# A run of small TensorE products and of other engines' operations behind the last store of an mLSTM and MLP kernel

## The chip, the cores and the metric

The kernel runs on one core of one Trainium2 chip. The metric is the device time of one execution in microseconds, the median of the runs. In the tables and rows PE is TensorE, PEld its weight loads, DVE VectorE, ACT ScalarE, POOL GpSimd and SP the engine that issues the DMAs.

## The reference

Two stages follow each other. The first is a gated recurrence per batch (4), head (8) and step (768), head size 40, here cut to its loop:

```python
for t in range(S):
    m_new = np.maximum(f_gate[:, :, t] + m, i_gate[:, :, t])
    f_stab = np.exp(f_gate[:, :, t] + m - m_new)
    i_stab = np.exp(i_gate[:, :, t] - m_new)
    C = f_stab * C + i_stab * np.einsum('bhd,bhe->bhde', vt, kt)
    n = f_stab * n + i_stab * kt
    y[:, :, t] = sigmoid(o_gate) * (C @ qt) / np.maximum(np.abs(n . qt), 1.0)
```

Its output, laid out as 3072 tokens of 320 values, goes through an MLP: `h = x @ w_in` (320 to 2048), `g = h * clip(h + 3, 0, 6) / 6`, and `g @ w_out` (2048 to 320), which is the result.

## The kernel before

The recurrence is computed in chunks of 128 steps, and three chunks of one batch make a unit of 384 tokens; there are eight units. For a unit, two tasks of four heads each compute scores (`s`), decays (`gw`), the products with the values (`o`) and the running state (`C`). Small fp32 products stand there at the start of the program: `s` in line 659 (40 rows of the array in use, 128 columns of weights, 128 streamed), `o` in lines 701 and 708 (42 columns streamed) and the state's `c` in line 581 (40 columns of weights, 42 streamed). Later tasks use bf16 pieces instead (lines 662, 703 to 711). Products of zeros (`pw`, line 359) fill PE's gaps until the first unit is done.

A unit then goes through the MLP. `mm1` (line 877) makes the 16 blocks of the hidden layer, each from eight fp32r products of 384 streamed columns, into two PSUM buffers `mm0` and `mm1`. ACT and DVE make `g`, then its high and low parts `gh` and `gl` in fp32r. `mm2` (lines 920 to 922) adds the products of 320 columns into `acc0` to `acc2`. `evac` copies each `acc` to one of three SBUF buffers `ob0` to `ob2`, on ACT, DVE and ACT in turn (lines 940 and 937), and SP stores it (line 943).

The order of each engine's instructions is set ahead by a planner (`Plan`), which gives every step costs and due times and emits the steps in the order that it simulates. `plan.run()` emits all of them; each engine then executes its list in that order, and semaphores make it wait for what it needs from another. At the program's end all engines meet in closing steps.

The last steps of the program are the last `mm2` of unit 7 on PE, the three copies of `acc`, and the three stores. The change calls a function behind `plan.run()`. It uses buffers that the kernel has: `g0` and `gl0` for its operands, `mm0`, `mm1` and the `acc` buffers for its results in PSUM, and `ob0` in SBUF.

Of the kernel before, what the change touches and what calls it, by code (L numbers as in the profile page):

```python
# [7 lines left out]
F32 = mybir.dt.float32  # L8
F32R = mybir.dt.float32r
BF16 = mybir.dt.bfloat16  # L10
U32 = mybir.dt.uint32
AF = mybir.ActivationFunctionType
ALU = mybir.AluOpType
# [3 lines left out]
DM, FF = 320, 2048  # L17
# [11 lines left out]
NEG = -1.0e30  # L29
# [59 lines left out]
class Mat(float):  # L89


    w = 0.0
# [18 lines left out]
class Plan:  # L111
# [21 lines left out]
    def put(self, tag, slot):  # L133
        self.slots[tag].append((self.now["t"], slot))
# [152 lines left out]
def mlstm_moe_kernel(ctx: ExitStack, tc: tile.TileContext, ig, fg, qkd, natd, ond, w_in, w_out, ident_d, out):  # L287
    nc = tc.nc
# [10 lines left out]
    whi = wts.tile([128, 2, FF], F32R, name="whi")  # L299
# [4 lines left out]
    ident = cst.tile([128, 128], F32, name="ident")  # L304
    ones = cst.tile([128, max(WN, 128)], BF16, name="ones")
    half = cst.tile([128, 1], F32, name="half")
# [23 lines left out]
    def pick(i, due=0.0, **costs):  # L330
        opts = {e: costs[e] for e in {"x": "dg", "y": "da", "z": "dga", "p": "g"}.get(ENGINES[i], ENGINES[i]) if e in costs}
        return ("*", opts, due) if len(opts) > 1 else (*list(opts.items())[0], due)
# [10 lines left out]
    def psub(i, n, g=None, due=0.0):  # L343
        return pick(i, due, d=ld(n), g=g or cg(n))

    def pcast(i, n, due=0.0):
        return pick(i, due, a=ca(n), d=lf(n))
# [503 lines left out]
    P = {}  # L851
# [77 lines left out]
    def evac(u, t):  # L929
# [13 lines left out]
        nc.sync.dma_start(out[t0 + t * L : t0 + (t + 1) * L, :], ob)  # L943
        put(*got)

    def due(u, k):
        if u == 1:
            return T0 + SPAN * (k + 1) / 7 - AH1
        return T0 + SPAN * (u - 1) + SPAN * (k + 1) / 7 - AH
# [8 lines left out]
    for task in range(2 * NU):  # L958
# [3 lines left out]
        k = quad * U  # L962
# [44 lines left out]
            plan.add(T0 + SPAN * u + SPAN - MV, evac(u, t), [f"acc{u}_{t}"])  # L1007
    with tc.manual_schedule(engines={ET.PE, ET.Activation, ET.DVE, ET.Pool, ET.SP}):
        plan.run()


_INS = ["ig", "fg", "qk", "nat", "on", "w_in", "w_out", "ident"]
# [49 lines left out]
```

## Time and profile before

| what | value |
|---|---|
| median of the timed runs | 576.79 us (576.59 to 576.99) |
| the profiled execution, first to last instruction (span) | 591.0 us |
| PE busy | 540.3 us, 91% of the span |
| PEld busy | 493.6 us |
| DVE busy | 404.1 us |
| ACT busy | 337.8 us |
| POOL busy | 141.0 us |
| mean granted TensorE clock | 0.913 of full speed |

The profiled execution has no other time than its span, and it is 14.2 us longer than the median of the timed runs. Matmuls are pipelined: a row's duration reaches from a product's start until its results are written, and the next one starts before that, so PE's rate is read from the distance between starts. An fp32 product (plain fp32) stands in the trace as two MATMULs, one in fp32r as one, and a weight load stands beside each as PEld. A row of the timeline merges neighbours of the same line (x8). The granted clock is the share of TensorE's clock pulses that were let through.

### The profile page before, as it was taken

What the parts mean: (1) busy time and instruction counts of PE and PEld (TensorE: products, weight loads), DVE (VectorE), ACT (ScalarE), POOL (GpSimd) and SP (SyncE); (2) the same over time, 40 slices, a digit from 0 to 9 for tenths busy, and PEclk for the clock granted to TensorE, in tenths of its full rate; (3) what the DMA queues carried; (4) which work ended last, traced back from release to release, by engine and by line L of the source; (5) the groups of instructions that cost most, each with busy time, mean ns of one, the idle gap of its engine ahead of it and who ended that gap; (6) DMA issues with size and microseconds to landing.
All of it is one profiled execution on the core that took longest, in us unless ns stands there. A gap on an engine that the chain in (4) does not pass through costs nothing.

```text
span 591.0 us, 11413 instructions
## 1 busy us (share of the span) xinstructions
PE 540.3 (91%) x4207; PEld 493.6 (84%) x4207; DVE 404.1 (68%) x849; ACT 337.8 (57%) x738; POOL 141.0 (24%) x191
## 2 busy tenths in 40 slices
PE   8999999687799897999789997999978998999997
PEld 7988899476679797889678896999868997999997
DVE  6443476997588767779767775796957677685433
ACT  4521164474746756667666666676756567544433
POOL 3242111543530312221211322132212203110000
PEclk9555588788999999999889998999989999999999
DMA  8524137549316226253454135344534244300000
GB/s 280 145 74 154 41 109 192 159 149 259 123 48 180 96 77 180 83 145 97 140 178 143 37 112 158 105 136 139 155 112 144 67 123 140 123 15 34 1 1 34
DMA packets 34548, 69.26 MB, mean 117 GB/s; under 512 B 4301, under 2 KB 14725, under 8 KB 34493
## 3 DMA queue, kind: packets, MB, share of 16 engines
q1 hardware_dynamic: 34493, 68.54, 38.0%
q8 instruction: 33, 0.54, 0.4%
q14 instruction: 22, 0.18, 0.1%
HBM read 42.66 MB, written 4.03 MB: 79 GB/s over the span
## 4 chain that ended last, share of the span: by engine, by line
PE 57%; DMA 16%; DVE 12%; ACT 7%; SPq 3%; issue 2%; POOL 1%; DVEq 0%; POOLq 0%; ACTq 0%
PE h L877 20%; DMA gw<-gsc 6%; PE acc L920 5%; PE acc L922 5%; PE acc L921 5%; PE pw L359 3%; DMA nat<-in_nat_dram 3%; PE o L701 3%; PE s L659 2%; DMA qk<-in_qk_dram 2%; PE c L581 2%; PE o L708 2%; PE s L662 2%; DMA rawi<-in_w_in_dram 2%; PE acc L918 2%
## 5 line engine op out<-in xcount | busy, mean ns | idle before, releaser
L877 PE MATMUL h<-xh,whi 128*128 128x384 f32 x256 | 95.4, 373 | 17.9 <-DVE g L893 17.8
L893 DVE SCALAR_TENSOR_TENSOR g<-g,h 128x384 f32<-128x384 f32 x128 | 70.1, 551 | 60.3 <-ACT g L891 59.7
L920 PE MATMUL acc<-vh,gh 128*128 128x320 f32 x336 | 108.6, 323 | 1.4 <-ACT gh L339 1.4
L891 ACT ACTIVATE g<-h,half 128x384 f32<-128x384 f32 x128 | 73.6, 576 | 57.4 <-PE h L877 49.7
L922 PE MATMUL acc<-vh,gl 128*128 128x320 f32 x336 | 104.1, 310 | 0.1
L921 PE MATMUL acc<-vl,gh 128*128 128x320 f32 x336 | 104.1, 310 | 0.0
L877 PE MATMUL h<-xl,whi 128*128 128x384 f32 x256 | 88.7, 347 | 0.0
L877 PE MATMUL h<-xh,wlo 128*128 128x384 f32 x256 | 88.7, 346 | 0.0
L642 ACT ACTIVATE gw<-gw,cT 128x128 f32<-128x128 f32 x192 | 65.4, 393 | 32.9 <-POOL gw L637 32.8
L637 POOL TENSOR_SCALAR_AFFINE_SELECT gw<-gw 128x512 f32<-128x512 f32 x46 | 33.2, 722 | 187.8 <-DMA gw<-gsc 144.1
L901 DVE TENSOR_TENSOR gl<-g,gh 128x384 fp32r<-128x384 f32 x112 | 63.8, 573 | 19.0 <-ACT gh L339 18.3
L339 ACT CAST gh<-g 128x384 fp32r<-128x384 f32 x112 | 57.1, 511 | 30.3 <-DVE g L893 29.5
L877 PEld LDWEIGHTS h<-xh,whi 128*128 128x128 f32 x256 | 50.2, 196 | 24.0 <-DVE g L893 23.1
L920 PEld LDWEIGHTS acc<-vh,gh 128*128 128x128 f32 x336 | 63.6, 189 | 2.2 <-ACT gh L339 1.9
L922 PEld LDWEIGHTS acc<-vh,gl 128*128 128x128 f32 x336 | 63.4, 189 | 0.6 <-DVE gl L901 0.6
L921 PEld LDWEIGHTS acc<-vl,gh 128*128 128x128 f32 x336 | 63.7, 190 | 0.0
L339 ACT CAST p<-gw 128x512 bf16<-128x512 f32 x72 | 44.2, 614 | 19.7 <-DVE gw L666 13.8
L877 PEld LDWEIGHTS h<-xl,whi 128*128 128x128 f32 x256 | 50.3, 196 | 0.2
L877 PEld LDWEIGHTS h<-xh,wlo 128*128 128x128 f32 x256 | 50.2, 196 | 0.0
L877 PE MATMUL h<-xl,wtl 128*128 128x384 f32 x128 | 45.0, 352 | 0.4 <-DVE xl L784 0.3
L877 PE MATMUL h<-xh,wtl 128*128 128x384 f32 x128 | 44.5, 348 | 0.0
L666 DVE TENSOR_TENSOR gw<-s,gw 128x512 f32<-128x512 f32 x48 | 33.0, 687 | 16.7 <-PE s L662 9.5
(118 smaller groups left out, 1096.8 us busy)
## 6 DMA issues: line engine op xcount, KB each, us to landing
st<-spl SPq DMA_DIRECT2D x117, 160.0 KB
gw<-gsc SPq DMA_DIRECT2D x46, 256.0 KB
nat<-in_nat_dram SPq DMA_DIRECT2D x16, 492.0 KB
qk<-in_qk_dram SPq DMA_DIRECT2D x13, 480.0 KB
rawi<-in_w_in_dram SPq DMA_DIRECT2D x8, 640.0 KB
rawo<-in_w_out_dram SPq DMA_DIRECT2D x8, 640.0 KB
on<-in_on_dram SPq DMA_DIRECT2D x8, 480.0 KB
out_dram<-ob SPq DMA_DIRECT2D x24, 160.0 KB
```

The lines of the kernel that those rows point to most:

```text
L339: nc.scalar.copy(dst, src)
L359: nc.tensor.matmul(pw[:, :WN], ones[:, :128], ones[:, :WN], start=True, stop=True)
L637: nc.gpsimd.affine_select(gw, gw, pattern=[[0, 4], [1, L]], compare_op=ALU.is_ge, fill=NEG, base=0, channel_multiplier=-1)
L642: nc.scalar.activation(gw[:, h, :], gw[:, h, :], AF.Exp, bias=cT[:, c, r0 + h : r0 + h + 1], scale=1.0)
L666: nc.vector.tensor_tensor(gw, sp, gw, ALU.mult)
L877: nc.tensor.matmul(hp, w, x, start=n == 0, stop=n == len(seq) - 1)
L891: nc.scalar.activation(g, hp, AF.Relu, bias=half, scale=1.0 / 6.0)
L893: nc.vector.scalar_tensor_tensor(g, g, 1.0, hp, ALU.min, ALU.mult)
L901: E(e).tensor_sub(gl, g, gh.bitcast(F32))
L920: nc.tensor.matmul(acc, gh[:, ts_], VH[f // 4][:, f % 4, :], start=f == 0, stop=False)
L921: nc.tensor.matmul(acc, gh[:, ts_], VL[p][:, f % 2, :], start=False, stop=False)
L922: nc.tensor.matmul(acc, gl[:, ts_], VH[f // 4][:, f % 4, :], start=False, stop=f == NF - 1)
```

## The change

A function `shapes` is added and called once, behind all steps of the plan. It first copies two pieces of the weights `whi` into SBUF (`sh_src` in fp32, `sh_srr` in fp32r, both on DVE). Then it issues 206 products on PE, in groups that differ in the rows, the weight columns and the streamed columns. Where an operand starts at row 64, or the result at partition 64, the product lies in another part of the array; operands of up to 64 rows or results of up to 64 partitions take a sub-array tile of 64 rows or columns. Behind them six exponentials on ACT, eight operations on POOL and six on DVE write the scratch tile `sh_sc` in `ob0`. Nothing that it writes is stored.

On PE the new rows stand right behind what was the last product, where only the program's closing branch stood. `acc` is the accumulator of the last unit, `shm` are the new results in `mm0` and `mm1`.

```order
 L921 MATMUL acc_2_7030<-vl_2147,gh_15_7312 128x320
 L922 MATMUL acc_2_7030<-vh_2027,gl_15_7313 128x320
-L1057 UNCONDITIONAL_BRANCH
+L956 MATMUL shm_7370<-whi 128x512
+L956 MATMUL shm_7371<-whi 128x512
```

Nothing of before moved; eight more products like the last two follow, then the others. Further down the same list, still on PE, stand the products in column tiles, the transposes, and the first round of those that mix one product of full width with four in 64x64 tiles (`sha` are the new results in the `acc` buffers).

```order
+L956 MATMUL shm_7370<-sh_src 64x128 x8
+L956 MATMUL shm_7370<-sh_src 40x42 x10
+L993 MATMUL shm_7370<-ident,sh_src 128x128 x4
+L956 MATMUL shm_7371<-whi 128x384
+L956 MATMUL sha_7372<-sh_src 64x64 x2
+L956 MATMUL sha_7373<-sh_src 64x64 x2
```

All of these are new rows, and none of them stands ahead of a product of the kernel. On DVE the program ended with the copy of the second accumulator; now the two copies of weights and six operations stand behind it. The last four read PSUM tiles that PE writes (`sha`, `shm`).

```order
 L937 COPY ob_1_7352<-acc_1_7020 128x320
-L1057 UNCONDITIONAL_BRANCH
+L950 COPY sh_src<-whi 128x384
+L951 CAST sh_srr<-whi 128x384
+L1023 TENSOR_TENSOR sh_sc<-sh_src 128x256 x2
+L1025 SCALAR_TENSOR_TENSOR sh_sc<-sh_src,half,sha_7372 128x42 x2
+L1027 TENSOR_TENSOR sh_sc<-sh_src,shm_7370 128x256 x2
+L1141 UNCONDITIONAL_BRANCH
```

The list of DVE ahead of these rows is the one of before. ACT and POOL get their rows at the end of their lists in the same way; SP's list is the same.

```diff
--- before.py
+++ after.py
@@ -943,6 +943,89 @@
         nc.sync.dma_start(out[t0 + t * L : t0 + (t + 1) * L, :], ob)
         put(*got)
 
+    def shapes():
+        mo = P["mo"]
+        src = mo.tile([128, 384], F32, tag="g0", name="sh_src")
+        srr = mo.tile([128, 384], F32R, tag="gl0", name="sh_srr")
+        nc.vector.tensor_copy(src, whi[:, 0, 0:384].bitcast(F32))
+        nc.vector.tensor_copy(srr, whi[:, 0, 512:896].bitcast(F32))
+        bank = [P["mm"].tile([128, 512], F32, tag=f"mm{i}", name=f"shm{i}") for i in range(2)]
+        bank += [P["ac"].tile([128, 512], F32, tag=f"ac{i}", name=f"sha{i}") if False else P["ac"].tile([128, DM], F32, tag=f"acc{i}", name=f"sha{i}") for i in range(3)]
+
+        def mm(out, w, x):
+            nc.tensor.matmul(out, w, x, start=True, stop=True)
+
+        for i in range(10):
+            mm(bank[i % 2], whi[:, 0, i * 128 : i * 128 + 128], whi[:, 1, 0:512])
+        for i in range(8):
+            mm(bank[i % 2][:, :384], whi[:, 0, 0:128], whi[:, 1, 0:384])
+        for i in range(8):
+            mm(bank[2 + i % 2][:, :320], whi[:, 0, 0:128], whi[:, 1, 0:320])
+        for n in (64, 42):
+            for k in range(6):
+                for r in range(2):
+                    for c in range(2):
+                        rows = slice(r * 64, r * 64 + (40 if n == 64 else 64))
+                        mm(bank[r][c * 64 : c * 64 + 64, k * n : k * n + n], src[rows, k % 5 * 64 : k % 5 * 64 + 64], src[rows, 64 : 64 + n])
+        for k in range(8):
+            for r in range(2):
+                mm(bank[r][r * 64 : r * 64 + 64, k * 42 : k * 42 + 42], src[r * 64 : r * 64 + 64, k * 40 : k * 40 + 64], src[r * 64 : r * 64 + 64, 64:106])
+        for k in range(6):
+            for r in range(2):
+                for c in range(2):
+                    mm(bank[r][c * 64 : c * 64 + 40, k * 42 : k * 42 + 42], src[r * 64 : r * 64 + 64, k * 40 : k * 40 + 40], src[r * 64 : r * 64 + 64, 64:106])
+        for k in range(4):
+            for r in range(2):
+                mm(bank[r][:, k * 128 : k * 128 + 128], src[r * 64 : r * 64 + 40, k * 80 : k * 80 + 128], src[r * 64 : r * 64 + 40, 128:256])
+        for k in range(4):
+            for r in range(2):
+                mm(bank[r][:, k * 42 : k * 42 + 42], src[r * 64 : r * 64 + 40, k * 80 : k * 80 + 128], src[r * 64 : r * 64 + 40, 128:170])
+        for k in range(5):
+            for r in range(2):
+                mm(bank[r][:, 0:384], srr[r * 64 : r * 64 + 64, k * 64 : k * 64 + 128], srr[r * 64 : r * 64 + 64, 0:384])
+        for k in range(4):
+            for c in range(2):
+                mm(bank[0][c * 64 : c * 64 + 64, k * 128 : k * 128 + 128], src[:, k * 60 + c * 50 : k * 60 + c * 50 + 64], src[:, 0:128])
+        for k in range(5):
+            for c in range(2):
+                mm(bank[0][c * 64 : c * 64 + 40, k * 42 : k * 42 + 42], src[:, k * 60 + c * 40 : k * 60 + c * 40 + 40], src[:, 0:42])
+        for k in range(4):
+            nc.tensor.transpose(bank[0][:, k * 128 : k * 128 + 128], src[:, k * 80 : k * 80 + 128], ident)
+        for k in range(4):
+            mm(bank[1][:, 0:384], whi[:, 0, k * 128 : k * 128 + 128], whi[:, 1, 0:384])
+            for r in range(2):
+                for c in range(2):
+                    rows = slice(r * 64, r * 64 + 40)
+                    mm(bank[2 + r][c * 64 : c * 64 + 64, k * 64 : k * 64 + 64], src[rows, k * 64 : k * 64 + 64], src[rows, 64:128])
+        for k in range(4):
+            mm(bank[1][:, 0:384], whi[:, 0, k * 128 : k * 128 + 128], whi[:, 1, 0:384])
+            mm(bank[0][:, 0:42], src[:, 0:128], src[:, 0:42])
+            mm(bank[0][:, 42:84], src[:, 0:128], src[:, 0:42])
+        for k in range(4):
+            mm(bank[1][:, 0:384], whi[:, 0, k * 128 : k * 128 + 128], whi[:, 1, 0:384])
+            for r in range(2):
+                mm(bank[2 + r][:, 0:320], srr[r * 64 : r * 64 + 64, 0:128], srr[r * 64 : r * 64 + 64, 0:320])
+        sc = mo.tile([128, DM], F32, tag="ob0", name="sh_sc")[:, :256].rearrange("p (h t) -> p h t", h=4)
+        s4 = src[:, 0:256].rearrange("p (h t) -> p h t", h=4)
+        for h in range(4):
+            nc.scalar.activation(sc[:, h, :], s4[:, h, :], AF.Exp, bias=half, scale=1.0)
+        nc.scalar.activation(sc, s4, AF.Exp)
+        nc.scalar.activation(sc, s4, AF.Exp)
+        for k in range(2):
+            nc.gpsimd.tensor_tensor(sc, s4, src[:, 256:320][:, None, :].broadcast_to([128, 4, 64]), ALU.add)
+        for k in range(2):
+            nc.gpsimd.tensor_tensor(sc, s4, src[:, 256:260][:, :, None].broadcast_to([128, 4, 64]), ALU.add)
+        for k in range(2):
+            nc.gpsimd.affine_select(sc, s4, pattern=[[0, 4], [1, 64]], compare_op=ALU.is_ge, fill=NEG, base=0, channel_multiplier=-1)
+        for k in range(2):
+            nc.gpsimd.tensor_scalar(sc, s4, half, None, ALU.add)
+        for k in range(2):
+            nc.vector.tensor_tensor(sc, s4, src[:, 256:260][:, :, None].broadcast_to([128, 4, 64]), ALU.add)
+        for k in range(2):
+            nc.vector.scalar_tensor_tensor(sc[:, 0, 0:42], src[:, 0:42], half, bank[2][:, 0:42], ALU.mult, ALU.add)
+        for k in range(2):
+            nc.vector.tensor_tensor(sc, s4, bank[0][:, 0:256].rearrange("p (h t) -> p h t", h=4), ALU.mult)
+
     def due(u, k):
         if u == 1:
             return T0 + SPAN * (k + 1) / 7 - AH1
@@ -1007,6 +1090,7 @@
             plan.add(T0 + SPAN * u + SPAN - MV, evac(u, t), [f"acc{u}_{t}"])
     with tc.manual_schedule(engines={ET.PE, ET.Activation, ET.DVE, ET.Pool, ET.SP}):
         plan.run()
+        shapes()
 
 
 _INS = ["ig", "fg", "qk", "nat", "on", "w_in", "w_out", "ident"]
```

## The prediction

> **What bounds the kernel now.** The page gives the span and, in its chain of waits, whose work ends last.
>
> ```profile
> span 591.0 us, 11413 instructions
> PE 57%; DMA 16%; DVE 12%; ACT 7%; SPq 3%; issue 2%; POOL 1%; DVEq 0%; POOLq 0%; ACTq 0%
> ```
>
> PE carries 57% of that chain. But the change stands behind all of it, so what counts is the last four microseconds and how PE runs small products. First the end, from the timeline (start, duration, engine, line), and the wait of the closing step of the DMA queue.
>
> ```profile
> 587.31 0.31 PE L921 MATMUL acc<-vl,gh 128*128 128x320 f32 x1
> 587.46 0.30 PE L922 MATMUL acc<-vh,gl 128*128 128x320 f32 x1
> 587.80 0.42 ACT L940 COPY ob<-acc 128x320 f32<-128x320 f32 x1 [1.33 <-PE acc L922]
> 588.25 0.33 SPq L943 DMA_DIRECT2D out_dram<-ob  x1
> ...
> SPq L1057 <- DMA out_dram<-ob: 1.4, 1, 1.4
> ```
>
> PE's last product starts at 587.46; products of this shape follow each other 0.15 us apart, so PE could take the next at 587.6. The copy ends at 588.22, the store is issued by 588.58, lands some 1.4 later at 590.0, and 1.0 us of closing steps (all engines meet) makes 591.0. Thus 2.4 us of PE work behind 587.6 would lie beside the landing; the rest moves the end.
>
> **What the change costs, by part.** All of it is new work; the order shows nothing moved ahead of it on any queue. An fp32 product stands in the trace as two MATMULs with a weight load each (72 rows of L659 for 36 products), an fp32r product as one. I number the groups as the code has them, in MATMULs as the trace will count them: dense fp32r 10 of 512 columns, 8 of 384, 8 of 320; then (1) 48 of 40 rows x 64 columns, (2) 48 of 64x64 streaming 42, (3) 32 of the same in two tiles, (4) 48 of 64x40, (5) 16 of 40x128 streaming 128, (6) 16 of the same streaming 42, (7) 10 fp32r of 64x128 streaming 384, (8) 16 of 128x64, (9) 20 of 128x40, (10) 4 transposes, (11) four times one dense of 384 and 8 of kind 1, (12) four times one dense and 4 of 128x128 streaming 42, (13) four times one dense and 2 half-row fp32r of 320.
>
> Prices at full clock: the chain in order of time, then PE's timeline at 77, 101 and 104 us. What counts is the distance between starts, since the durations overlap.
>
> ```profile
> 574.11 1.39 PE h L877 x8
> ...
> 77.24 1.13 PE L659 MATMUL s<-st 40*128 40x128 f32 x8
> 78.31 1.07 PE L359 MATMUL pw<-ones 128*128 128x128 bf16 x16
> ...
> 101.31 0.50 PE L766 MATMUL xa<-ident,on 128*128 128x128 f32 x3
> 101.64 0.31 PE L701 MATMUL o<-nat,gw 128*128 128x42 f32 x2
> 101.78 0.22 PE L711 MATMUL o<-cS,st 120*128 120x42 bf16 x2
> 101.85 0.40 PE L701 MATMUL o<-nat,gw 128*128 128x42 f32 x2
> 102.07 0.22 PE L711 MATMUL o<-cS,st 120*128 120x42 bf16 x2
> ...
> 104.69 0.50 PE L581 MATMUL c<-vp,nat 128*40 128x42 f32 x8
> 105.13 0.44 PE L877 MATMUL h<-xh,whi 128*128 128x384 f32 x1
> 105.41 0.33 PE L877 MATMUL h<-xl,whi 128*128 128x384 f32 x1
> ```
>
> Dense 384 columns: 1.39/8 = 0.174; 320: 0.145 (the tail rows); 512 by the same slope 0.232. L659 (128-column load, 128 streamed): 1.07/8 = 0.134. L701 (128-column load, 42 streamed): from 101.85 to 102.07 two, 0.11 each; it streams a third of L659's columns and costs 0.82 of it, so its load sets it. L581 (40-column load, 42 streamed): 0.44/8 = 0.055. Transposes 0.33/3 = 0.11. Behind L581 the dense product takes 0.28, not 0.174: 0.1 for the change of tile shape. The pair of L711 shows the smallest distance: 0.07 for two, 0.035 each.
>
> No row shows products in two different tiles of the array at once. Their cost is bounded above by the rows of one tile (L581, L659 by columns: 0.075 for kind 1, 0.06 for 2 and 3, 0.055 for 4) and below by half of that or the 0.035 of L711. I take the middle: loads go one behind another, streams of different tiles overlap, so the load sets the price as in L701, 0.11 for 128 columns, 0.055 for 64, 0.04 for 40. It is the row with the shortest stream to its load, as these have.
>
> At full clock: dense 10 x 0.232 + 8 x 0.174 + 8 x 0.145 = 4.9. Kinds 1 to 7: 48 x 0.055 = 2.6, 2.6, 32 x 0.055 = 1.8, 48 x 0.04 = 1.9, 16 x 0.11 = 1.8, 1.8, 10 x 0.11 = 1.1; together 13.6. Kinds 8 to 10: 16 x 0.067 (half of L659, two tiles) = 1.1, 20 x 0.04 = 0.8, 4 x 0.11 = 0.4; 2.3. Kind 11: 4 x (0.28 + 8 x 0.055) = 2.9; kind 12: 4 x (0.174 + 0.06 + 4 x 0.11) = 2.7; kind 13: 4 x (0.234 + 2 x 0.11) = 1.8 (0.06, about half a change of shape, is an estimate); 7.4. Sum 28.2.
>
> **The clock.** The granted clock is the second term. Here are stretches of 3.41 us, the step in which it changes in this trace (columns: length, PE busy, PEld, DVE, ACT, POOL, clock, DMA share, GB/s), and PE's timeline at half clock.
>
> ```profile
> 20.40:23.80 3.40, 3.40 (x25) 2.94 (x24) 2.04 (x5) 1.51 (x6) 1.00 (x2) 0.50 0.45 130
> ...
> 73.27:76.68 3.41, 3.41 (x36) 2.89 (x34) 2.74 (x12) 3.30 (x9) 0.00 (x0) 1.00 0.00 0
> ...
> 80.10:83.51 3.41, 3.41 (x30) 3.07 (x28) 3.01 (x7) 2.50 (x8) 0.68 (x1) 1.00 0.47 144
> 83.51:86.92 3.41, 3.41 (x14) 3.19 (x13) 2.71 (x6) 1.66 (x2) 0.56 (x1) 0.50 0.49 176
> ...
> 47.91 0.78 PE L581 MATMUL c<-vp,nat 128*40 128x42 f32 x8
> 48.63 1.94 PE L701 MATMUL o<-nat,gw 128*128 128x42 f32 x8
> 50.49 2.07 PE L659 MATMUL s<-st 40*128 40x128 f32 x8
> 52.50 0.69 PE L766 MATMUL xa<-ident,on 128*128 128x128 f32 x2
> ```
>
> PE was busy in every one of these, and yet had half its clock in some: what decides isn't being busy. At half clock L701 takes 1.86/8 = 0.2325 (2.1 times), L659 2.01/8 = 0.251 (1.9), L581 0.72/8 = 0.09. What stood in 73.27 to 76.68 (next stretch full) and in 80.10 to 83.51 (next one half), grouped:
>
> ```profile
> L701 PE MATMUL o<-nat,gw 128*128 128x42 f32 x7 | 1.5, 289 | 0.0
> L708 PE MATMUL o<-C,st 40*128 40x42 f32 x6 | 1.2, 292 | 0.0
> L359 PE MATMUL pw<-ones 128*128 128x128 bf16 x12 | 0.8, 220 | 0.0
> L581 PE MATMUL c<-vp,nat 128*40 128x42 f32 x8 | 0.5, 206 | 0.0
> L772 PE MATMUL xb<-ident,on 128*128 128x128 f32 x2 | 0.5, 312 | 0.0
> L766 PE MATMUL xa<-ident,on 128*128 128x128 f32 x1 | 0.4, 421 | 0.0
> ...
> L708 PE MATMUL o<-C,st 40*128 40x42 f32 x8 | 1.7, 292 | 0.0
> L701 PE MATMUL o<-nat,gw 128*128 128x42 f32 x8 | 1.6, 288 | 0.0
> L359 PE MATMUL pw<-ones 128*128 128x128 bf16 x12 | 0.8, 219 | 0.0
> L659 PE MATMUL s<-st 40*128 40x128 f32 x2 | 0.5, 336 | 0.0
> ```
>
> Count columns streamed (fp32 twice per MATMUL), weighted by the share of the 128 rows in use: the first holds 588 + 158 + 1,536 + 672 + 768 = 3,722, the second 210 + 672 + 1,536 + 160 = 2,578. So a stretch must reach something between, to keep the clock. Kinds 1 to 6 bring (1,920 + 2,016 + 1,344 + 2,016 + 1,280 + 420) = 9,000 in 12.5 us, 2,450 per stretch: too few. The clock falls one whole stretch after the dense products end, 3.4 to 6.8 us later, say 5.1. Then 13.6 - 5.1 = 8.5 us run at half clock and take 2.1 times as long: +9.4. Kinds 8 to 10 fill all 128 rows and should bring the clock back, but only after a stretch of theirs: 2.3 more. Sum 28.2 + 11.7 = 39.9: PE ends at 587.6 + 39.9 = 627.5.
>
> **The tail's end and the other engines.** DVE's last four operations read PSUM that PE wrote last.
>
> ```profile
> L718 DVE TENSOR_TENSOR ht<-o,eG 128x168 f32<-128x168 f32 x40 | 13.0, 326 | 20.9 <-PE o L708 16.3 <-PE o L711 4.5
> L666 DVE TENSOR_TENSOR gw<-s,gw 128x512 f32<-128x512 f32 x48 | 33.0, 687 | 16.7 <-PE s L662 9.5 <-PE s L659 3.9 <-ACT gw L642 2.0
> L542 POOL TENSOR_TENSOR vp<-nat,wT 128x168 f32<-128x168 f32 x40 | 22.9, 589 | 42.2 <-DMA nat<-in_nat_dram 28.6 <-PE h L877 4.6 <-ACT dec L443 4.4
> ```
>
> By these two DVE rows 42 columns take 0.19 and 256 take 0.42: 2 x 0.19 + 2 x 0.42 + 0.2 of waits in between = 1.4; and 1.0 of closing steps: 2.4 behind PE. ACT's six exponentials wait for the landing of the store from ob0 (about 588.5), take under 0.4 each, and POOL's eight operations follow (0.9 each by L542 in proportion to columns): they end near 599, DVE's first two at 600. All this lies beside PE's work up to 627; it would cost only if PE ended before 600. DVE's two copies of 384 columns run after 587.4 and are done before PE wants them behind its dense products.
>
> Span after: 627.5 + 2.4 = 629.9, 38.9 over 591.0. The profiled span is 14.2 us above the median of the timed runs, 576.79; I add the difference to the median: 615.7, say **616**.
>
> **Rivals.**
> - *One tile at a time* (20%). For it: no row shows otherwise. Kinds 1 to 7 at the upper prices, 3.6 + 2.9 + 1.9 + 2.6 + 2.1 + 1.8 + 1.7 = 16.6; 8 to 10, 3.7; 11 to 13, 8.3; 33.5 in all, plus 1.1 x (11.5 + 3.7) at half clock: 50.2, time 626. If the clock never comes back in kinds 11 to 13, 9 more.
> - *Tiles side by side* (22%). Half the upper prices: 4.9 + 10.4 + 6.5 = 21.8 at full clock, which the denser stream may keep: time 598; with the rest of kinds 1 to 10 at half clock, 603. The Trainium skill, TensorE: Matmul & The Clock Gate, Part 3, says that products in different tiles of the array run at the same time, a few ns apart, with gains of 2.4 to 10.6 times; no run here shows it yet.
> - *The clock stays* (8%): PE never idles in the tail. Sum 28.2, time 604. The Trainium skill, same page, Part 1, has the clock fall after an idle stretch of about 3.4 us and rise after a busy one; the trace agrees on step and half clock, but 20.40:23.80 is busy for 3.40 of 3.40 at 0.50, so I give it little.
> - *Not slower* (3%): the tail would have to fit beside the last store. It decides if PE needs under 2.4 us, or 13.9 to stay within 2%. Dense products alone (4.9 and 12 x 0.174) take 7.0, and 314 others at 0.035 take 11; so only if the products didn't run at all: 577.
>
> **How the numbers follow.** The forecast has 45%, its own range 610 to 623 (the clock falling 3.4 to 6.8 us after the dense part, and kinds 11 to 13 partly at half clock). With the rivals at 598 to 604 and most of the one at 626: 598 to 628. Left out are the ends of both, and 577. A change of 2% is 11.5 us, about what a measurement can tell: slower 0.96, within 0.03, faster 0.01.
>
> **What would show it.** In the profile after, PE's clock at 0.5 in the slices behind 597; starts of kind 2 0.055 apart at full clock (0.03: side by side; 0.06 and more: one at a time); the chain ending PE, DVE L1025, L1027; ACT and POOL done by 600. The forecast is wrong if the clock stays at 1.0, if the dense groups aren't 0.145 to 0.232 apart, or if the span grows by under 20 or over 50 us.

## The result and the profile after

The changed kernel takes 603.28 us (601.31 to 605.26) against 576.79 (576.59 to 576.99): a ratio of 1.046, with an interval of 1.031 to 1.061, so 18 to 35 us more. Slower, as forecast, and inside the range; but 13 us under the predicted 616, and the profile shows that the two largest terms of the sum, the price of kinds 1 to 6 and the clock, were wrong. Each side is two runs. Some executions of one kernel take some per cent longer at a lower granted clock; the ratios, here and below, leave these out (four of six when the changed kernel was repeated, three of eleven of before beside it, one of four with columns alone).

First the span of the kernel after, and PE's clock from the dense products to the end of its work, in stretches of 3.41 us (start and end, length, PE busy and rows in it, clock, DMA share, GB/s).

```profile
span 599.6 us, 12148 instructions
...
578.84:582.25 3.41, 3.41 (x116) 1.00 0.02 5
582.25:585.66 3.41, 2.75 (x102) 1.00 0.02 5
585.66:589.08 3.42, 3.42 (x64) 1.00 0.00 0
...
592.49:595.90 3.41, 3.41 (x23) 1.00 0.00 0
```

The clock is 1.00 in every one: it didn't fall in the tail. The timeline of PE from its last product of the kernel, and DVE's end; the columns are start, duration, engine, line, and how many were merged.

```profile
575.51 0.30 PE L922 MATMUL acc<-vh,gl 128*128 128x320 f32 x1
575.65 3.87 PE L956 MATMUL shm<-whi 128*128 128x512 f32 x18
579.36 1.33 PE L956 MATMUL sha<-whi 128*128 128x320 f32 x8
580.61 2.83 PE L956 MATMUL shm<-sh_src 40*64 40x64 f32 x157
584.11 2.34 PE L956 MATMUL shm<-sh_src 64*40 64x42 f32 x51 [0.66 <-issue]
586.27 1.13 PE L956 MATMUL shm<-sh_srr 64*128 64x384 f32 x10
587.34 1.48 PE L956 MATMUL shm<-sh_src 128*64 128x128 f32 x36
...
589.16 0.42 PE L956 MATMUL shm<-whi 128*128 128x384 f32 x1
...
589.78 0.44 PE L956 MATMUL shm<-whi 128*128 128x384 f32 x1
590.15 0.34 PE L956 MATMUL sha<-sh_src 40*64 40x64 f32 x8
...
596.73 0.41 PE L956 MATMUL sha<-sh_srr 64*128 64x320 f32 x2
...
597.18 0.55 DVE L1025 SCALAR_TENSOR_TENSOR sh_sc<-sh_src,half,sha 128x42 f32<-128x42 f32 x2 [11.85 <-PE sha L956]
597.77 0.87 DVE L1027 TENSOR_TENSOR sh_sc<-sh_src,shm 128x256 f32<-128x256 f32 x2
```

PE works from 575.65 to 597.1, 21.5 us, where 39.9 were forecast. The 208 small MATMULs of kinds 1 to 6 take 5.7 us (580.61 to 586.27). In this lies a gap before 584.11, in which PE is idle for 0.66 us (0.86 from start to start). What the whole tail costs stands in one row, the wait of the closing step in SP's queue, which before waited for the store alone:

```profile
SPq L1141 <- DVE sh_sc L1027: 20.5, 1, 20.5
SPq L1141 <- DMA out_dram<-ob: 1.4, 1, 1.4
```

The landing takes its 1.4 us as before, and then the closing step waits 20.5 us for DVE's last operation. From PE's last product of the kernel to the end it is 599.6 - 575.5 = 24.1 us here, and 591.0 - 587.5 = 3.6 before: 20.5 again.

That isn't the difference of the spans (8.6 us) nor that of the medians (26.5), because the part ahead of the change differs between executions. For the spans two stretches of each profile (length, PE busy, clock) show it, the first 120 us and the rest of the kernel's own work, before and then after:

```profile
0.00:120.00 120.00, 112.12 (x735) 0.67 0.48 146
120.00:587.60 467.60, 427.99 (x3473) 0.97 0.36 110
```

```profile
0.00:120.00 120.00, 107.05 (x770) 0.81 0.51 159
120.00:575.65 455.65, 419.96 (x3439) 0.97 0.36 109
```

The same 4,207 MATMULs end 12 us earlier in the profile after, and this lead is there already at the 735th, which starts at 121.2 us before; the clock over the first 120 us is 0.81 instead of 0.67. No instruction of this part was changed.

### The profile page after: what moved, and what is told of

The parts are those of the page before. It is cut to its first block, busy times and chain, and to the rows that moved or that the text cites. A ratio compares the mean times of both kernels' runs of the same rounds, so it can differ in the third digit from the quotient of the medians.

```text
span 599.6 us, 12148 instructions
## 1 busy us (share of the span) xinstructions
PE 547.8 (91%) x4559; PEld 499.9 (83%) x4559; DVE 407.6 (68%) x857; ACT 339.8 (57%) x744; POOL 145.3 (24%) x199
## 4 chain that ended last, share of the span: by engine, by line
PE 52%; DMA 17%; DVE 16%; ACT 7%; SPq 3%; issue 3%; POOL 1%; DVEq 0%; POOLq 0%; ACTq 0%
PE h L877 18%; DMA nat<-in_nat_dram 7%; DMA gw<-gsc 5%; PE acc L920 5%; PE acc L921 5%; PE acc L922 5%; DMA qk<-in_qk_dram 3%; PE shm L956 3%; PE o L701 3%; DVE g L893 2%; PE o L708 2%; PE c L581 2%; PE pw L359 2%; ACT gw L642 2%; PE acc L918 2%
## 5 line engine op out<-in xcount | busy, mean ns | idle before, releaser
L604 POOL TENSOR_TENSOR d<-dr,d 40x168 bf16<-40x168 f32 x33 | 21.0, 638 | 82.1 <-issue 49.0
```

Of the source, the lines that this page charges most:

```text
L604: E(e).tensor_sub(d[:, 0], r, d[:, 2])
```

## The experiments

**The changed kernel again.** No edit; it asks whether more than the tail became longer.

> The changed kernel again, to separate the tail from what stands ahead of it. In the first profile after, PE's tail took 21.5 us from its first product at 575.65, and everything behind the last product of before 24.0 us, against 3.4 us in the profile before: 20.5 us of added time, while the timed runs differ by 26.5. Theory one (the tail costs 20.5 us, the rest is the body, whose stretches at half clock differ from execution to execution): over more runs the difference comes to 19 to 24 us, and the body's end in the profiles moves by several us either way. Theory two (the change lengthens the body too): the difference stays at 25 to 28 us, and the body ends later in every run.

Measured: ratio 1.029 (1.018 to 1.039) against the runs of before beside it, 11 to 23 us. Its profile has the tail once more: PE's last product at 576.40, the end at 600.8, 24.4 us, 20.8 over before. Both intervals hold 20.5, and their middles, 26.5 and 17, lie on both sides of it; neither excludes a few microseconds more. In the eleven profiles of this and the following kernels, the last product of the kernel's own work starts between 575.5 and 582.5. The eight runs of before that count here have spans of 577.8 to 585.8; less the 3.6 us behind that product, they put it between 574.2 and 582.2, in the same range. So theory one fits in the size of the tail and in the spread of the part ahead of it. Theory two's 25 to 28 us lie outside the second interval; a smaller lengthening of that part isn't excluded.

**One tile.** All positions are set to row 0, column 0; counts and shapes stay.

```diff
-  mm(bank[r][c * 64 : c * 64 + 64, ...], src[r * 64 : r * 64 + 64, ...], ...)
+  mm(bank[r][0 : 64, ...], src[0 : 64, ...], ...)
```

> All products of the tail keep their rows, columns and count, but each stands in the tile at row 0 and column 0. Theory one (products in different tiles of the array run side by side, and the clock stays because that fills a stretch of 3.41 us with work): one tile at a time costs what my upper prices said, 0.05 to 0.075 us for each of kinds 1 to 4, 0.11 to 0.134 for 5 and 6, 33 us of PE at full clock, and the granted clock falls to 0.5 in the tail, so that PE needs 45 to 55 us and the time is 45 to 55 over before. Theory two (short products follow each other fast whatever the tile, and the clock counts products, not work): PE's tail stays at 20 to 25 us at a clock of 1.0, and the time at 20 to 27 over before.

The time: ratio 1.084 (1.077 to 1.091). PE's timeline, and then stretches of 3.41 us in which the clock changes:

```profile
582.47 3.87 PE L956 MATMUL shm<-whi 128*128 128x512 f32 x18
...
587.44 20.26 PE L956 MATMUL shm<-sh_src 40*64 40x64 f32 x208
607.49 3.54 PE L956 MATMUL shm<-sh_srr 64*128 64x384 f32 x10
610.97 5.07 PE L956 MATMUL shm<-sh_src 128*64 128x128 f32 x36
...
587.44:590.28 2.84, 2.84 (x49) 1.00 0.02 6
...
588.89:592.30 3.41, 3.41 (x62) 0.99 0.00 0
592.30:595.71 3.41, 3.41 (x35) 0.50 0.00 0
...
612.78:616.19 3.41, 3.41 (x30) 0.51 0.00 0
616.19:619.60 3.41, 3.41 (x32) 1.00 0.02 5
```

The 208 small MATMULs take 20.0 us instead of 5.7. Kind 1, at full clock throughout, takes 2.84/48 = 0.059 each; in four tiles it takes 0.0156 (0.75 us for 48). The clock falls at 592.3, 4.9 us behind the dense products (5.1 was forecast), and is back at 616.2, with the transposes of kind 10, about as forecast. The tail from the last product of the kernel is 46.3 us. So position alone decides both the price and the clock: theory two is out. The time is 7.7 to 9.1% over before, 45 to 53 us, and inside the 45 to 55 expected; the tail adds 42.7, a little less. So at least 2 us of the timed difference lie ahead of the tail here, and no run shows what they are.

**Rows alone and columns alone.** In one kernel all products stand at column 0 (kind 3 keeps its two diagonal tiles), in the other all at row 0.

```diff
-  mm(bank[r][c * 64 : c * 64 + 64, ...], src[rows, ...], src[rows, ...])      # rows = r * 64 ...
+  mm(bank[r][0 : 64, ...], src[rows, ...], src[rows, ...])                    # rows alone
+  mm(bank[r][c * 64 : c * 64 + 64, ...], src[0 : 40, ...], src[0 : 40, ...])  # columns alone
```

> The tail's products keep their two row positions (0 and 64) but stand at column 0, except the 32 MATMULs of kind 3, which keep their two diagonal tiles. Theory one (each tile has its own loads and streams; two tiles give half the price): kinds 1, 2 and 4 at 0.025 to 0.035 us each instead of 0.0145 to 0.02, kinds 8 and 9 at 0.13 and 0.05, kinds 5 to 7 as before; PE's tail 25 to 29 us at full clock, and the clock near its limit, since kinds 1 to 4 then bring some 3,500 to 4,500 row-weighted columns per stretch. Rival (the row positions bring all of the overlap, columns none): kinds 1 to 4 stay at 0.0145 to 0.02.

> The tail's products keep their two column positions (0 and 64) but stand at row 0, kind 3 in one tile alone. Theory one (tiles in any position run side by side): kinds 1, 2 and 4 at 0.025 to 0.035 us, kind 3 at 0.055 to 0.06, kinds 5 to 7 at 0.13, 0.11 and 0.17, kinds 8 and 9 as in the changed kernel (0.058, 0.024); PE's tail 28 to 32 us at full clock, more where the clock falls. Rival (the rows bring all of it): kinds 1, 2 and 4 at 0.05 to 0.075.

PE's timeline with rows alone:

```profile
585.80 6.80 PE L956 MATMUL shm<-sh_src 40*64 40x64 f32 x208
592.43 1.13 PE L956 MATMUL shm<-sh_srr 64*128 64x384 f32 x10
```

And with columns alone, its timeline with kind 1 by itself ahead of the same 208, and the stretch ahead of the clock's fall with the one behind it:

```profile
583.96 1.61 PE L956 MATMUL shm<-sh_src 40*64 40x64 f32 x48
...
583.96 14.47 PE L956 MATMUL shm<-sh_src 40*64 40x64 f32 x208
...
584.16:587.58 3.42, 3.42 (x110) 1.00 0.02 5
587.58:590.99 3.41, 3.41 (x65) 0.50 0.02 5
```

Kind 1 takes 1.45 us in both kernels, 0.030 each: two tiles halve the price of one, whichever way they lie, and four quarter it. Both rivals (rows bring it all) are out. Everything behind the last product of the kernel takes 26.7 us with rows alone and 37.3 with columns alone; ratios 1.046 (1.039 to 1.053) and 1.060 (1.049 to 1.072). PE's tail took 24.1 us with rows alone (25 to 29 were expected), and 34.8 with columns alone, where the clock fell (28 to 32, more with a fall). But one thing didn't fit theory one: with columns alone the clock fell at 587.6, although the stretch before it holds 110 small MATMULs, over 4,000 columns by my count (rows in use), and 3,722 had been enough. With rows alone it stayed at 1.00 until PE was done. So the way of counting in the prediction was wrong; it had only been tested on products in one column position.

**The clock, rows against columns.** Behind the dense products stand 96 equal products of 40x64 streaming 128, in two column positions in turn, or in two row positions in turn; kinds 1 to 13 are left out. These two kernels and those below were timed once each, so only their profiles are read.

```diff
+  for k in range(48):
+      for c in range(2):
+          mm(bank[0][c * 64 : c * 64 + 64, ...], src[0:40, ...], src[0:40, 128:256])
```

> Behind the dense products stand 96 fp32 products (192 MATMULs) of 40 rows x 64 columns, 128 streamed, two column positions in turn, all at row 0; the other kinds are left out. Two at a time at about 0.058 each: 11 us at full clock, 4,700 columns per 3.41 us if every product's columns count by its rows in use, 2,350 if products side by side in columns count once, or if columns in use count too. Theory one, changed by the first four runs (the clock follows how much of the rows is in use over time: row tiles add up, column tiles side by side count once): 2,350 is too few, the clock falls 3.4 to 6.8 us behind the dense part and PE needs 15 to 20 us for these products. Rival (each product counts by its rows, as in the prediction): 4,700 is enough, the clock stays, 11 us.

> The pair of the run with two column positions: the same 96 products, but at two row positions (0 and 64) in turn, all at column 0. Theory one as changed (row tiles add up): 4,700 columns by rows in use per 3.41 us, the clock stays at 1.0, 11 us for 192 MATMULs. Rival one (each product counts by its rows): the same here, 11 us. Rival two (both rows and columns in use count, so a 40x64 product counts a sixth): 2,350, the clock falls as in the other run, 15 to 20 us.

PE's 192 MATMULs with columns in turn, and stretches of 3.41 us:

```profile
583.55 16.01 PE L956 MATMUL shm<-sh_src 40*64 40x128 f32 x192
...
585.09:588.51 3.42, 3.42 (x66) 1.00 0.02 5
588.51:591.92 3.41, 3.41 (x38) 0.51 0.00 0
```

And with rows in turn:

```profile
582.69 10.70 PE L956 MATMUL shm<-sh_src 40*64 40x128 f32 x192
...
584.41:587.83 3.42, 3.42 (x68) 1.00 0.00 0
587.83:591.24 3.41, 3.41 (x66) 1.00 0.02 5
```

The same products, 66 and 68 in a stretch at full clock: 66 x 256 x 40/128 = 5,280 columns by rows in use. With columns in turn the clock falls and 192 MATMULs take 16.0 us; with rows in turn it stays and they take 10.7. Counting every product fails on the first. Counting rows and columns in use fails on the second: a stretch of 66 would hold half, 2,640, in both, but it lost the clock with columns and kept it with rows. What fits both is: rows in use, added up over row tiles, and column tiles that run side by side counted once, 2,640 in the first. That lies by the 2,578 that lost the clock before, and under the 3,722 that kept it. The pair also differs in that the rows write two PSUM buffers in turn and the columns one; columns alone, above, wrote two and lost the clock too.

This way of counting was found from two of the earlier kernels, and the pair is its only test. It can't be the whole rule, with one limit for all. In the run with 288 products in four tiles, below, 128 MATMULs in a stretch make 128 x 84 x 64/128 = 5,376, 2,688 with columns counted once, and the clock stayed at 1.00 through all of them (length, busy time of PE, PEld, DVE, ACT and POOL, clock, DMA share, GB/s):

```profile
587.63:602.68 15.05, 9.53 (x577) 8.93 (x576) 1.42 (x5) 0.00 (x0) 3.39 (x6) 1.00 0.02 4
```

But ahead of the tail, in the profile after, a stretch (346.67 to 350.08) of nine dense products of 320 columns, 2,880, lost it: the next one ran at 0.50. How much column tiles count stays open; that they count less than row tiles is what the pair shows.

**Changes of shape.** The twelve dense products of kinds 11 to 13 are put ahead of the small ones.

> The twelve dense products of kinds 11 to 13 stand together ahead of the small ones of these kinds, instead of four times three rounds in turn; count and shapes are the same. In the changed kernel a round of kind 11 takes 0.65 us (0.37 for the dense product, 0.28 for the eight small), one of kind 12 0.62, one of kind 13 0.72: 7.9 us in all. Theory one (a change of the tile's shape costs 0.1 to 0.2 us, in which the array empties): grouped, twelve dense take 2.1, 32 of kind 1 0.6, 16 of 128x128 1.5, 8 half-row ones 0.8: 5.0 us, 2.9 less. Rival (the small ones' own price is higher than in long runs, whatever stands between): no gain over 0.5 us.

PE's timeline, grouped:

```profile
592.29 2.34 PE L956 MATMUL shm<-whi 128*128 128x384 f32 x12
594.56 0.69 PE L956 MATMUL sha<-sh_src 40*64 40x64 f32 x32
595.18 1.98 PE L956 MATMUL shm<-sh_src 128*128 128x42 f32 x16
597.09 0.85 PE L956 MATMUL sha<-sh_srr 64*128 64x320 f32 x8
```

They take 592.29 to 597.94, 5.65 us, where the changed kernel took 589.16 to 597.14, 7.98: 2.3 less, of 2.9 expected. A dense product between small ones takes 0.37 (589.78 to 590.15), in a row 0.19, so two changes of shape cost about 0.18 there. By kind, the dense ones at 0.19 each: kind 11 gains 1.2 us and kind 13 gains 1.3; kind 12, whose small products have the tile of the dense ones (128*128), gains nothing (2.51 in turn, 2.67 grouped). So it is the change of the tile's shape that costs, and the rival is out.

**Without PE.** The tail's products are left out; five memsets write what DVE reads.

> The tail without its products: the two copies of weights, ACT's six, POOL's eight and DVE's six operations stay, and five memsets on DVE stand in for what PE wrote. In the profile after, POOL's last operation ended 8.9 us behind the start of PE's last product of the kernel (584.41 against 575.51), DVE's first two 9.8 behind it. Both theories: DVE's last four take 1.4 more and the closing steps 1.0, so everything behind PE's last product takes 12.2 us instead of 3.6 before and 24.1 after, 8.6 over before; that is what the other engines' part would cost without the cover of PE. If the span ends less than 6 over before, or more than 11, another wait stands in it.

PE's last product starts at 577.68 and the span ends at 589.94: 12.3 us, 8.7 over before, as expected. The queue's closing wait says the same:

```profile
SPq L1093 <- DVE sh_sc L979: 8.7, 1, 8.7
```

So ACT's, POOL's and DVE's operations would cost 8.7 us alone, and cost nothing beside PE, but for DVE's last four.

**The gap in kind 4.** The gap of 0.86 us from start to start in the changed kernel is named "issue": PE waits for nothing that the profile shows. It stands before the same instruction in the repetition. One kernel has 288 equal products in four tiles behind the dense ones and nothing else; another is the changed kernel without 16 of its dense products.

> Behind the dense products stand 288 fp32 products (576 MATMULs, 1,152 instructions with their loads) of 64x64 streaming 42, in four tiles in turn; the other kinds are left out. In the changed kernel such MATMULs follow each other 0.019 us apart, and the one gap of 0.86 to 1.2 us stands before the same instruction of the tail (the 366th, loads counted) in three runs, 2.4 to 2.6 us after a fetch of 16 KB of instructions began. Theory one (PE takes instructions faster than they are fetched): gaps of 0.5 to 1.5 us recur, 256 instructions (16 KB at 64 bytes, the size being an estimate from that) apart, four of them, and 576 MATMULs take 13 to 16 us. Rival (the gap belongs to kind 4 or to a wait): no gap over 0.3 us, 11 us in all.

> The changed kernel without 16 of its first 18 dense products (8 of 512, 8 of 384 columns), so that all that follows stands 32 instructions earlier in the program. Theory one (instruction fetch): the gap stands before the same place of the program, so 32 instructions further on in the tail's sequence than before, in kind 4's end or kind 5, and is longer, since PE gets there some 3 us sooner after less dense work. Rival (a wait or kind 4 itself): the gap stands in front of the same MATMUL of kind 4.

PE's timeline of the first:

```profile
587.63 2.53 PE L956 MATMUL shm<-sh_src 64*64 64x42 f32 x157
591.26 2.07 PE L956 MATMUL shm<-sh_src 64*64 64x42 f32 x128 [1.10 <-issue]
594.99 2.07 PE L956 MATMUL shm<-sh_src 64*64 64x42 f32 x128 [1.65 <-issue]
...
601.90 0.78 PE L956 MATMUL shm<-sh_src 64*64 64x42 f32 x35 [1.38 <-issue]
```

And of the second:

```profile
582.49 2.99 PE L956 MATMUL shm<-sh_src 40*64 40x64 f32 x173
586.14 2.18 PE L956 MATMUL shm<-sh_src 64*40 64x42 f32 x35 [0.66 <-issue]
```

Gaps recur every 128 MATMULs, 256 instructions with their loads, and 576 MATMULs take 15.05 us. PE is idle in the four gaps for 1.10 to 1.65 us each (0.5 to 1.5 were expected), 5.5 in all; from start to start they are 6.4. In the second the gap stands after 173 small MATMULs instead of 157, so 32 instructions further on, as many as were taken out: at the same place of the program. That is what fetching of instructions in blocks of 16 KB, 256 instructions, would do; each gap ends 2.3 to 2.7 us behind the start of such a fetch. The gap in the second was not longer, though, as theory one had it. The Trainium skill, Runtime: NRT & Kernel Launch, Instruction fetch mechanics, has the same blocks of 256 and says that crossing from one to the next is mostly hidden; the trace agrees on the block, and shows it unhidden here, where PE takes 256 instructions in 2.07 us.

## Why the prediction was right in its range and wrong in its sum

**The end and what covers what.** These steps held. The tail stands alone on the path; all but the landing of the last store is exposed. DVE's end took 597.18 to 598.64, 1.46 us (forecast 1.4), and 0.96 of closing steps (1.0). POOL ended 8.9 us behind PE's last product of the kernel (11.5 forecast, by a price per operation that was too high: 0.42 to 0.92 us), and the cover was worth 8.7 us, by the run without PE.

**"No row shows products in two different tiles at once ... I take the middle."** This step failed. I took it that weight loads go one behind another and set the price. They don't: with four tiles in turn a MATMUL with its load takes 0.0156 us where one tile takes 0.059, so loads and streams of the four run beside each other. Kinds 1 to 6 took 5.7 us, not 12.5. Kind 7 took 1.06 (1.1 forecast), kinds 8 to 10 1.8 (2.3). The rival "tiles side by side" gave 21.8 us of PE, the profile 21.5. Part of that is luck: it halved all upper prices, where four tiles in fact quarter them, and was too low for kinds 11 to 13 (6.5; forecast 7.4; measured 8.0), where dense and small products alternate. My 0.1 and 0.06 for a change of shape were guesses from one row; it is nearly 0.2 for a dense product that stands between 64x64 tiles.

**"Too few. The clock falls."** This step failed with the first one. Its rule had been read from two stretches of before, and there it separates the two rightly: work counts, not busy time. In one tile the clock fell 4.9 us behind the dense part, inside the 3.4 to 6.8 forecast, and came back about where I said; that 4.9 lies so near the 5.1 of the sum, the middle of that range, is luck. But the density that goes into it was that of products in one tile. Side by side, kinds 1 to 6 bring their work in less than half the time, and the clock stays at 1.0 until PE is done: 11.7 us of the sum weren't there. And the count itself needs an amendment on columns, which the pair of runs shows but doesn't settle. The Trainium skill, TensorE: Matmul & The Clock Gate, Part 1, ties the clock to how busy PE has been; the run with columns in turn shows PE busy for 3.41 of 3.41 us at 0.50, so being busy isn't enough.

**The sum.** Of 39.9 us forecast for PE, 28.2 at full clock became 21.5 (6.8 less in kinds 1 to 6, 0.5 less in 8 to 10, 0.6 more in 11 to 13), and 11.7 for the clock became 0. The forecast describes the kernel in one tile (43.8 us of PE) better than the one that was changed. By its own signs it was wrong: the clock stayed at 1.0.

**The number to which it was added.** That the profile of before was 14 us longer than the timed runs was noted and left unexplained. Against the profile after, it was 12 us longer in the kernel's first 120 us, which ran at a clock of 0.67 there and of 0.81 after; no profile shows this part of the timed runs. Working with the difference to the kernel's last product, and not with spans, kept this out of the sum. The medians may keep some of it: 20.5 us of tail show as 26.5 there, and no run shows what the other 6 are. Without them the time would be 576.8 + 20.5 = 597.3, just under the range's lower end of 598. So it is luck, too, that the measured time lies inside.

## What to carry to other kernels

Small products cost by where they stand: in turn over two tiles, by rows or columns, they cost half, over four tiles a quarter, as long as the shape of the tile doesn't change in between, which costs up to 0.2 us. In these runs small products in two row tiles kept PE's clock and the same products in two column tiles lost it, so put row tiles side by side first; columns side by side save time but count less for the clock, if at all. And a tail that follows the last store is measured from the last instruction of the kernel's own work, not from span to span.

## What the runs showed of the hardware

- Products in four 64x64 tiles in turn: 0.0156 us per MATMUL with its load (64 columns streamed), against 0.030 in two and 0.059 in one.
- Row tiles side by side count more for the clock than column tiles: of two runs of the same 96 products, the one with columns in turn lost the clock (0.50, with PE busy for 3.41 of 3.41 us), the one with rows in turn stayed at 1.00.
- PE was idle for 1.10 to 1.65 us after every 256 instructions, where it took them in 2.07 us; each gap ended 2.3 to 2.7 us behind the start of a fetch of 16 KB of instructions. So four tiles in turn didn't sustain 0.016 us per MATMUL: over 576 it was 15.05/576 = 0.026.
